# A fused long convolution and maxout FFN: the input's transposes moved from TensorE to the DMA engines

## The chip, the cores and the metric

The kernel runs on one core of a Trainium2 chip. The metric is the device time of one execution in microseconds, the median of several runs. A core has five engines with a queue of instructions each: TensorE (PE, matrix products; its weight loads are listed apart as PEld), VectorE (DVE), ScalarE (ACT), GpSimd (POOL) and SyncE (SP, which here only issues transfers). Sixteen DMA engines carry the transfers. Engines run side by side and wait for one another through semaphores.

## The reference, cut to what matters

```python
def _attn_ref(x, v, pos_emb, w1, w2):             # x, v: (4, 12544, 128)
    h_mlp = np.maximum(pos_emb @ w1, 0.0) @ w2    # a filter per channel
    window = np.exp(-0.01 * np.arange(S))[:, None]
    h_filt = h_mlp * window
    u = x * v
    Uf = np.fft.rfft(u, n=2 * S, axis=1)
    Hf = np.fft.rfft(h_filt, n=2 * S, axis=0)
    y = np.fft.irfft(Uf * Hf[None], n=2 * S, axis=1)[:, :S, :]
    return x * y

def _moe_ref(x, w1, w2, w3, w_out):               # x: (50176, 128), w1..w3: (128, 768)
    h = np.maximum(np.maximum(x @ w1, x @ w2), x @ w3)
    return h @ w_out
```

A causal convolution along the sequence of each channel of `u = x * v`, gated with x, goes through an FFN whose hidden value is the maximum of three products. All arrays are fp32.

## The kernel before

The kernel does the Fourier transforms as matrix products. The 12544 = 128 x 98 positions of a channel lie in a tile as 128 partitions by 98. The first product of the transform contracts over the 98, so each 128 x 98 block is first transposed. A *u* is a set of four channels of one batch, 32 u to a batch. Its steps: load x and v (`u_load`), multiply (`u_mul`), transpose four blocks on TensorE into PSUM and copy them out with ScalarE (`u_turn`), and the first product in two halves (`u_first`).

```python
    def u_load(b, u):
        c, g0 = divmod(u, NG // 4)
        ts = []
        for src in (xr, vr):
            t = (inp0 if b == 0 and u % 2 else inp).tile([P, 4, NB], FP32, tag=f"u{len(ts)}", name="ut")
            nc.sync.dma_start(
                t[:], src[4 * g0:4 * g0 + 4, :, c, b, :].rearrange("g p n -> p g n"))
            ts.append(t)
        us[u] = ts

    def u_mul(u):
        a, v = us[u]
        nc.vector.tensor_tensor(out=a[:], in0=a[:], in1=v[:], op=ALU.mult)

    def turn(u, ps):
        a, _ = us.pop(u)
        for i in range(4):
            nc.tensor.transpose(ps[0:NB, i * P:(i + 1) * P], a[:, i, :], eye[:])

    def u_turn(u):
        if u % 2 == 0:
            uts[u] = uts[u + 1] = utp.tile([NB, 8, 2, 64], FP32, tag="uT", name="uT")
        ps = state["turn"].tile([P, 512], FP32, tag="cv", name="pst")
        turn(u, ps)
        nc.scalar.copy(uts[u][:, 4 * (u % 2):4 * (u % 2) + 4],
                       ps[0:NB, :].rearrange("n (s t r) -> n s r t", s=4, r=2))

    def u_first(u, h, copy=None):
        t = uts[u] if h == 0 else uts.pop(u)
        ps = cps.tile([P, 512], FP32, tag="cv", name="ps1")
        at = 4 * u + 2 * h
        first_halves(ps, [t[:, at % 8 + j] for j in range(2)], f1[:], spec[:, :, :, at:at + 2],
                     copy or copies[h])
```

The convolution of batch 0 is a stage of its own, with the first six u of batch 1 at its end. Then come four batches of FFN tiles, 32 tiles of six steps f each, and beside the FFN of batch b runs the convolution of batch b + 1. `conv_steps` lays it out over the 192 steps (slots) of a batch: first the 32 u (26 for batch 1), then the 45 pairs g of frequencies. An instruction stands in its engine's queue in the order in which the slots name it.

```python
    def conv_steps(b, done):


        out = []

        def at(slot, late, fn, *args):
            out.append((slot, late, len(out), fn, args))

        per_pair = 172 / (NK + 0.4 * (NU - done))
        for u in range(done, NU, 2):
            s = (u - done) * 0.4 * per_pair + 6
            for v in range(2):
                at(max(0, int(s) - 6), 0, u_load, b, u + v)
                at(int(s) - 2 + v, 0, u_mul, u + v)
                at(int(s), 1, u_turn, u + v)
                for h in range(2):
                    at(int(s + 1 + 0.2 * per_pair * (2 * v + h)), 1, u_first, u + v, h)
        s0 = int((NU - done) * 0.4 * per_pair) + 7
        for g in range(NK):
            s = s0 + int(g * per_pair)
            at(s - 5, 0, w_load, g, 0)
            at(s - 3, 0, h_load, g)
            at(s, 1, g_second, g)
            at(s + 1, 0, w_load, g, 1)
            at(s + 1, 0, g_butterfly, g)
            at(s + 2, 0, g_swap, g)
            at(s + 3, 0, g_re, g)
            at(s + 4, 0, g_im, g)
            at(s + 5, 0, g_unfold, g)
            at(s + 6, 1, g_third, b, g)
        slots = {}
        for s, _, _, fn, args in sorted(out, key=lambda r: r[:3]):
            slots.setdefault(s, []).append((fn, args))
        return slots
```

The FFN side: loads for a tile two tiles ahead, and the order of its steps.

```python
    def t_load(b, i):
        zt = hp.tile([N1, 2, 512], FP32, tag="zt", name="zt", bufs=2)
        if b == 0:
            nc.sync.dma_start(
                zt[:], zd[b][:, :, 2 * i:2 * i + 2, :].rearrange("k c t f -> k c (t f)"))
        else:
            for c in range(2):
                nc.sync.dma_start(
                    zt[NK * c:NK * c + NK],
                    zd[b].rearrange("(g a) c t f -> g a c t f", a=2)[
                        :, :, c, 2 * i:2 * i + 2, :].rearrange("g a t f -> g a (t f)"))
        zts[b, i] = zt
        xT = hp.tile([D, 4, NB], FP32, tag="xT", name="xT", bufs=2)
        for c in range(GC):
            nc.sync.dma_start(xT[c * NG:(c + 1) * NG], x[:, 4 * i:4 * i + 4, c, b, :])
        xTs[b, i] = xT
    ...
    def up(i, f):
        rhs = gs[i][:].rearrange("d p n -> d (p n)")
        h = hp.tile([P, N], FP32, tag="hid", name="hid")
        pa = hps.tile([P, 512], FP32, tag="hps", name="pa")
        halves_mm(pa[:, 0:N], w_sb[1][:, f * P:(f + 1) * P], rhs, True, True)
        nc.scalar.activation(h[:], pa[:, 0:N], Relu)
        pb = hps.tile([P, 512], FP32, tag="hps", name="pb")
        halves_mm(pb[:, 0:N], w_sb[2][:, f * P:(f + 1) * P], rhs, True, True)
        nc.vector.tensor_tensor(out=h[:], in0=h[:], in1=pb[:, 0:N], op=ALU.max)
        return h
    ...
    hp = ctx.enter_context(tc.tile_pool(name="hp", bufs=3))
    f4p = hp.tile([N1, 2, NB // 2], FP32, name="f4p", bufs=1)
    nc.scalar.dma_start(f4p[:], f4p_d)
    op_ = ctx.enter_context(tc.tile_pool(name="op", bufs=2))
    wp = ctx.enter_context(tc.tile_pool(name="wp", bufs=3))
    hh = ctx.enter_context(tc.tile_pool(name="hh", bufs=4))
    cvp = ctx.enter_context(tc.tile_pool(name="cvp", bufs=3))
    cps = ctx.enter_context(tc.tile_pool(name="cps", bufs=4, space=PSUM))
    hps = ctx.enter_context(tc.tile_pool(name="hps", bufs=3, space=PSUM))
    ops = ctx.enter_context(tc.tile_pool(name="ops", bufs=1, space=PSUM))
    state = {"turn": cps, "pair": (wp, hh), "cv": (cvp, cps), "xb": 3}


    tiles = [(b, i) for b in range(B) for i in range(NT)]
    late = None
    for n, (b, i) in enumerate(tiles):
        if i == 0:
            beside = {}
            if b + 1 < B:
                beside = conv_steps(b + 1, EARLY if b == 0 else 0)
        if n == 0:
            t_load(*tiles[0])
            t_load(*tiles[1])
            t_last(tiles[0])
        for f in range(NF):

            if i < NT - 2:
                if f == 0:
                    t_load(*tiles[n + 2])
            elif i == NT - 1 and f < 2 and n + 1 + f < len(tiles):
                t_load(*tiles[n + 1 + f])
            h = up((b, i), f)
            if late is not None:
                down(*late)
```

A tile pool with `bufs=3` has three buffers for a tag; the fourth tile of that tag waits until the first one has been used for the last time.

Of the kernel before, what the change touches and what calls it, by code (L numbers as in the profile page):

```python
# [8 lines left out]

FP32 = mybir.dt.float32  # L10
I32 = mybir.dt.int32
ALU = mybir.AluOpType
ACTF = mybir.ActivationFunctionType
PSUM = bass.MemoryType.PSUM
P = 128
# [54 lines left out]
def kernel(  # L70
# [15 lines left out]
    nc = tc.nc  # L86
    NG, _, _, B, NB = x.shape
# [37 lines left out]
    copies = (nc.scalar.copy, nc.vector.tensor_copy)  # L125
# [8 lines left out]
    def first_halves(ps, lhs, table, dst, copy):  # L134


        for i, a in enumerate(lhs):
            for r in range(2):
                for c in range(2):
                    nc.tensor.matmul(  # L140
                        ps[64 * c:64 * c + 64, 256 * i + r * N1:256 * i + (r + 1) * N1],
                        a[:, r, :], table[:, c * N1:(c + 1) * N1],
                        start=(i % 2 == 0 and r == 0), stop=True, skip_group_check=True)
        copy(dst, ps[:].rearrange("p (s m) -> p s m", m=256)[:, :, 0:2 * N1].rearrange(  # L144
            "p s (r k) -> p k r s", r=2))
# [8 lines left out]
    def butterfly(ps, eo, xs):  # L154
        v = ps[:, :].rearrange("p (k r d) -> p k r d", k=2, r=2)
        nc.vector.tensor_tensor(out=xs[:, :, 0, :], in0=eo[:], in1=v[:, :, 0, :], op=ALU.add)
        nc.vector.tensor_tensor(out=xs[:, :, 1, :], in0=eo[:], in1=v[:, :, 0, :],  # L157
                                op=ALU.subtract)

# [10 lines left out]
    def scratch(name, bufs):  # L170
        return sml.tile([P, 2 * HF], I32, tag=name, name=name, bufs=bufs)[:]

    def load_raw(i, h, eng):
        r = scratch("raw", 2)
        if i < 3:
            src = (moe_w1, moe_w2, moe_w3)[i].bitcast(I32).rearrange("(g c) f -> c g f", c=GC)
            for c in range(GC):
                eng.dma_start(r[c * NG:(c + 1) * NG],
                                  src[c][:, h * 2 * HF:(h + 1) * 2 * HF])
        else:  # L180
            src = moe_w_out.bitcast(I32).rearrange("(c p) d -> p c d", p=P)
            eng.dma_start(r.rearrange("p (c d) -> p c d", c=NF // 2),
# [3 lines left out]
    def convert(r, i, h):  # L186
# [12 lines left out]
            lambda: two(out=f2_, in0=lo, scalar1=9, scalar2=ONE,  # L199
                        op0=ALU.logical_shift_right, op1=ALU.bitwise_or),  # L200
            lambda: two(out=f1_, in0=hi, scalar1=12, scalar2=9,
                        op0=ALU.logical_shift_left, op1=ALU.logical_shift_right),
            lambda: one(f1_, f1_, ONE, op=ALU.bitwise_or),
            lambda: two(out=ex, in0=hi, scalar1=1, scalar2=21,
                        op0=ALU.logical_shift_left, op1=ALU.logical_shift_right),
            lambda: two(out=ex, in0=ex, scalar1=896, scalar2=0,
# [16 lines left out]
    utp = ctx.enter_context(tc.tile_pool(name="utp", bufs=2))  # L223
# [91 lines left out]
    NU = NG  # L315
    us, uts, ws, hts, eos, xts, xss, abs_, pss = ({} for _ in range(9))
# [20 lines left out]
    def u_turn(u):  # L337
        if u % 2 == 0:
# [3 lines left out]
        nc.scalar.copy(uts[u][:, 4 * (u % 2):4 * (u % 2) + 4],  # L342
                       ps[0:NB, :].rearrange("n (s t r) -> n s r t", s=4, r=2))

    def u_first(u, h, copy=None):
        t = uts[u] if h == 0 else uts.pop(u)
        ps = cps.tile([P, 512], FP32, tag="cv", name="ps1")
# [3 lines that stand above are left out]
# [69 lines left out]
# [8 lines that stand above are left out]


        per_pair = 172 / (NK + 0.4 * (NU - done))  # L430
        for u in range(done, NU, 2):
            s = (u - done) * 0.4 * per_pair + 6
            for v in range(2):
                at(max(0, int(s) - 6), 0, u_load, b, u + v)
                at(int(s) - 2 + v, 0, u_mul, u + v)
                at(int(s), 1, u_turn, u + v)
                for h in range(2):
                    at(int(s + 1 + 0.2 * per_pair * (2 * v + h)), 1, u_first, u + v, h)
        s0 = int((NU - done) * 0.4 * per_pair) + 7
        for g in range(NK):  # L440
            s = s0 + int(g * per_pair)
            at(s - 5, 0, w_load, g, 0)
# [13 lines that stand above are left out]
# [50 lines left out]
# [10 lines that stand above are left out]
# [68 lines left out]
    for f in range(0, FO, 4):  # L584
        quad([hs[:, f + i] for i in range(4)], f1h[:], specH[:, :, :, f:f + 4])
        u, k = divmod(f // 4, 4)
# [10 lines left out]
    for u in range(0, NU, 2):  # L597
        t = uts.pop(u)
        for v in range(2):
            if u + 4 < NU:  # L600
                u_mul(u + 4 + v)
            at = 4 * (u + v)
# [66 lines left out]
    for s in range(NK + 3):  # L669
# [29 lines left out]
        if NK <= s < NK + 2:  # L699
            for v in range(4):  # L700
                u_first(2 * (s - NK) + v // 2, v % 2, nc.scalar.copy)
# [8 lines left out]
    for u in (4, 5):  # L710
        for h in range(2):
            u_first(u, h)
# [3 lines left out]
    hp = ctx.enter_context(tc.tile_pool(name="hp", bufs=3))  # L716
    f4p = hp.tile([N1, 2, NB // 2], FP32, name="f4p", bufs=1)
    nc.scalar.dma_start(f4p[:], f4p_d)
    op_ = ctx.enter_context(tc.tile_pool(name="op", bufs=2))
    wp = ctx.enter_context(tc.tile_pool(name="wp", bufs=3))  # L720
    hh = ctx.enter_context(tc.tile_pool(name="hh", bufs=4))
# [9 lines left out]
# [19 lines that stand above are left out]
            late = ((b, i), f, h)  # L750
            if f == 3 and n + 1 < len(tiles):
                t_last(tiles[n + 1])
            s = i * NF + f
            run(beside.pop(s, ()))
            if s == NT * NF - 1:
                assert not beside, sorted(beside)
# [38 lines left out]
```

## Time and profile before

| | |
|---|---|
| median of 3 runs | 2464.02 us (2463.47 to 2464.71) |
| span of the profiled execution | 2462.5 us |
| PE busy | 2445.7 us, 99% |
| DVE busy | 1343.9 us, 55% |
| ACT busy | 1010.5 us, 41% |
| POOL busy | 62.5 us, 3% |
| TensorE clock granted | 0.999 of full speed |
| DMA | 384.61 MB, mean 156 GB/s |
| `pst` transposes (line 335) | 512 on PE, 273 ns median each, overlapped |
| copy of `pst` by ACT (line 342) | 96 of 98x512 fp32, 588 ns each |

A row of the profile names the line of the kernel, the engine, the operation, the tile written and the tiles read with their shapes, how often it ran, its busy time and the mean of one. PE has its work overlapped, so a matmul's duration is longer than its share of the span; the chain that ended last gives that share. "Issue to landing" is the time from the moment a queue begins to issue a transfer until all of it has arrived. "Idle before" is the time in which an engine waited ahead of an instruction, with the releaser it waited for.

### The profile page before, as it was taken

To read this page: it belongs to the slowest core of one execution; us is meant where nothing else is said; L and a number is where in the kernel's file an instruction comes from. 1 tells how busy PE (TensorE), PEld (TensorE's weight loads), DVE (VectorE), ACT (ScalarE), POOL (GpSimd) and SP (SyncE) were. 2 spreads that over 40 slices of the span, in tenths; PEclk is the share of its full clock that TensorE was granted. 3 is DMA by queue.
4 is the path that set the end of the run, shared out by engine and by line. 5 is a ranking of instruction groups with operands and counts; after the bars stand their busy time and mean duration, and the time that the engine had idled before them with its cause. 6 is when DMAs were issued, how large, how long until landed. Compare 5 with 4: busy or idle time off the path is not lost.

```text
span 2462.5 us, 63180 instructions
## 1 busy us (share of the span) xinstructions
PE 2445.7 (99%) x26449; PEld 1476.2 (60%) x26449; DVE 1343.9 (55%) x2764; ACT 1010.5 (41%) x1981; POOL 62.5 (3%) x121
## 2 busy tenths in 40 slices
PE   8999999999999999999999999999999999999999
PEld 7988866655555556655555556655555554444444
DVE  5588833466666634366666743456766652222322
ACT  2688833334444433344444433344444432222222
POOL 2022200000000000000000000000000000000000
PEclk9999999999999999999999999999999999999999
DMA  7779855677777545577777735477777732222221
GB/s 160 182 240 274 265 127 122 166 200 192 193 185 205 145 105 121 124 197 201 209 207 200 201 86 133 115 186 198 206 206 203 204 105 55 64 58 57 61 55 36
DMA packets 449511, 384.61 MB, mean 156 GB/s; under 512 B 295204, under 2 KB 341341, under 8 KB 449225
## 3 DMA queue, kind: packets, MB, share of 16 engines
q1 hardware_dynamic: 326720, 291.64, 46.6%
q10 hardware_dynamic: 117129, 74.31, 10.1%
q0 software_dynamic: 5376, 14.62, 2.1%
q8 instruction: 208, 3.41, 0.6%
q14 instruction: 78, 0.64, 0.1%
HBM read 295.76 MB, written 84.67 MB: 154 GB/s over the span
## 4 chain that ended last, share of the span: by engine, by line
PE 98%; DVE 1%; issue 0%; ACT 0%; ACTq 0%; DVEq 0%
PE ops L131 24%; PE pa L131 21%; PE pb L131 20%; PE ps L131 13%; PE ps L140 7%; PE yps L131 5%; PE sps L654 3%; PE pst L335 3%; PE gps L640 1%; PE pm L302 1%; PE pw L131 1%; ACT ht L659 0%; DVE xs L391 0%; DVE zs L416 0%; DVE xt L392 0%
## 5 line engine op out<-in xcount | busy, mean ns | idle before, releaser
L514 DVE TENSOR_TENSOR hid<-hid,pb 128x392 f32<-128x392 f32 x768 | 431.3, 562 | 775.9 <-PE pb L131 462.7
L511 ACT ACTIVATE hid<-pa 128x392 f32<-128x392 f32 x768 | 382.5, 498 | 634.6 <-PE pa L131 600.0
L131 PE MATMUL pa<-gt,w_sb 128*64 128x392 f32 x3072 | 639.4, 495 | 0.7 <-DVE gt L499 0.7
L131 PE MATMUL ops<-hid,wo_sb 128*64 128x392 f32 x3072 | 637.6, 494 | 0.1
L131 PE MATMUL pb<-gt,w_sb 128*64 128x392 f32 x3072 | 635.8, 492 | 1.8 <-ACT hid L511 1.8
L131 PEld LDWEIGHTS pb<-gt,w_sb 128*64 128x64 f32 x3072 | 219.2, 137 | 289.2 <-issue 270.4
L131 PEld LDWEIGHTS ops<-hid,wo_sb 128*64 128x64 f32 x3072 | 215.9, 137 | 291.8 <-issue 232.6
L131 PEld LDWEIGHTS pa<-gt,w_sb 128*64 128x64 f32 x3072 | 198.8, 137 | 160.4 <-issue 101.0
L131 PEld LDWEIGHTS ps<-ab,wt 128*64 128x64 f32 x2880 | 167.1, 137 | 56.5 <-issue 33.7
L140 PEld LDWEIGHTS ps<-f,uT 98*64 98x64 f32 x4096 | 172.9, 137 | 36.5 <-issue 33.4
L131 PE MATMUL ps<-ab,wt 128*64 128x128 f32 x2880 | 189.5, 274 | 0.9 <-DVE ab L398 0.6
L131 PE MATMUL ps<-spec,wt 128*64 128x128 f32 x2880 | 187.9, 273 | 0.0
L140 PE MATMUL ps<-f,uT 98*64 98x90 f32 x4096 | 181.3, 241 | 0.0
L131 PEld LDWEIGHTS ps<-spec,wt 128*64 128x64 f32 x2880 | 163.8, 137 | 6.0 <-issue 5.6
L381 ACT ACTIVATE xs<-xt 64x512 f32<-64x512 f32 x180 | 113.1, 628 | 127.1 <-DVE xt L157 120.7
L144 ACT COPY spec<-ps 128x360 f32<-128x360 f32 (+1 forms) x132 | 71.6, 545 | 171.6 <-PE ps L140 171.4
L162 ACT COPY eo<-ps 128x256 f32<-128x256 f32 x180 | 67.1, 373 | 173.8 <-PE pa L131 150.8
L398 DVE TENSOR_TENSOR ab<-xt 128x256 f32<-128x256 f32 x360 | 136.0, 419 | 1.6
L387 DVE TENSOR_TENSOR xt<-xt,ht 128x512 f32<-128x512 f32 x180 | 123.5, 686 | 14.4 <-ACT ht L659 14.1
L392 DVE TENSOR_TENSOR xt<-xt,xs 128x512 f32<-128x512 f32 x180 | 124.6, 692 | 6.3
L416 DVE TENSOR_TENSOR zs<-ps,z 128x256 f32<-128x256 f32 x270 | 101.8, 419 | 47.4 <-ACT z L414 45.4
L131 PEld LDWEIGHTS yps<-f4p,zt 90*64 90x64 f32 x3072 | 106.1, 138 | 35.6 <-issue 34.0
(81 smaller groups left out, 1744.4 us busy)
## 6 DMA issues: line engine op xcount, KB each, us to landing
wt<-wt_const SPq DMA_DIRECT2D x360, 256.0 KB, 4.5
ht<-hd SPq DMA_DIRECT2D x270, 256.0 KB, 5.1
zd<-zs ACTq DMA_DIRECT2D x180, 256.0 KB, 4.3
zt<-zd SPq DMA_DIRECT2D x192, 180.0 KB, 3.8
ut<-in_xr_dram SPq DMA_DIRECT2D x128, 196.0 KB, 3.8
ut<-in_vr_dram SPq DMA_DIRECT2D x128, 196.0 KB, 4.1
xT<-in_x_dram SPq DMA_DIRECT2D x512, 49.0 KB, 3.1
out_dram<-ot ACTq DMA_DIRECT2D x128, 196.0 KB, 3.9
```

Source lines behind the costliest of these rows:

```text
L131: nc.tensor.matmul(out[64 * h:64 * h + 64], lhsT[:, 64 * h:64 * h + 64], rhs, start=start, stop=stop, skip_group_check=True)
L140: nc.tensor.matmul(ps[64 * c:64 * c + 64, 256 * i + r * N1:256 * i + (r + 1) * N1], a[:, r, :], table[:, c * N1:(c + 1) * N1], start=(i % ...
L144: copy(dst, ps[:].rearrange("p (s m) -> p s m", m=256)[:, :, 0:2 * N1].rearrange("p s (r k) -> p k r s", r=2))
L335: nc.tensor.transpose(ps[0:NB, i * P:(i + 1) * P], a[:, i, :], eye[:])
L381: nc.scalar.mul(xs[0:64], xt[64:128], -1.0)
L387: nc.vector.tensor_tensor(out=xt[:], in0=xt[:], in1=hts[g][:, 0], op=ALU.mult)
L392: nc.vector.tensor_tensor(out=xt[:], in0=xt[:], in1=xs[:], op=ALU.add)
L398: nc.vector.tensor_tensor(out=ab[:, :, q, :], in0=y[:, :, 0, :], in1=y[:, :, 1, :], op=op)
L416: nc.vector.tensor_tensor(out=zs[:, a], in0=ps[:, 0:256], in1=z1[:], op=op)
L511: nc.scalar.activation(h[:], pa[:, 0:N], Relu)
L514: nc.vector.tensor_tensor(out=h[:], in0=h[:], in1=pb[:, 0:N], op=ALU.max)
L654: nc.tensor.matmul(ps[64 * h:64 * h + 64, (2 * c + k) * 2 * D:(2 * c + k + 1) * 2 * D], G[:, k, c], w2x[:].rearrange("p s d -> p (s d)"), ...
```

## The change: the transposes beside the FFN by DMA

Beside the FFN the four TensorE transposes of a u are replaced. The transposing DMA works here on 2-byte elements, so GpSimd takes the fp32 product apart into a plane of low and a plane of high 16-bit halves (`u_planes`), each padded from 98 to 128 columns; one transposing DMA on SyncE's queue turns the eight 128 x 128 blocks (`u_dma`); ScalarE puts the low halves and VectorE the high halves back into the fp32 tile (`u_join`). The bits are kept as they are. Batch 0 and the first six u of batch 1 stay on TensorE. Each u is now laid out by itself rather than in pairs, with leads for the new steps. It is meant to relieve TensorE of work that isn't part of the products.

```diff
--- before.py
+++ after.py
@@ -9,6 +9,7 @@
 
 FP32 = mybir.dt.float32
 I32 = mybir.dt.int32
+U16 = mybir.dt.uint16
 ALU = mybir.AluOpType
 ACTF = mybir.ActivationFunctionType
 PSUM = bass.MemoryType.PSUM
@@ -342,6 +343,32 @@
         nc.scalar.copy(uts[u][:, 4 * (u % 2):4 * (u % 2) + 4],
                        ps[0:NB, :].rearrange("n (s t r) -> n s r t", s=4, r=2))
 
+
+
+    def u_planes(u):
+        a, _ = us.pop(u)
+        pl_ = planes[u % 2]
+        nc.gpsimd.tensor_copy(
+            pl_[:, :, :, 0:NB], a[:].bitcast(U16).rearrange("p s (n h) -> p h s n", h=2))
+        us[u] = pl_
+
+    def u_dma(u):
+        t = hp.tile([P, 8, P], U16, tag="turned", name="turned", bufs=2)
+        nc.sync.dma_start_transpose(
+            out=t[:], in_=us.pop(u)[:].rearrange("p h s n -> p (h s n)"))
+        us[u] = t
+
+    def u_join(u):
+        if u % 2 == 0:
+            uts[u] = uts[u + 1] = utp.tile([NB, 8, 2, 64], FP32, tag="uT", name="uT")
+        t = us.pop(u)
+        for h in range(2):
+            copies[h](
+                uts[u][:, 4 * (u % 2):4 * (u % 2) + 4].rearrange(
+                    "n s r t -> n (s r t)").bitcast(U16).rearrange(
+                    "n (s r t h) -> n h s r t", h=2, r=2, t=64)[:, h],
+                t[0:NB, 4 * h:4 * h + 4].rearrange("n s (t r) -> n s r t", r=2))
+
     def u_first(u, h, copy=None):
         t = uts[u] if h == 0 else uts.pop(u)
         ps = cps.tile([P, 512], FP32, tag="cv", name="ps1")
@@ -428,15 +455,16 @@
 
 
         per_pair = 172 / (NK + 0.4 * (NU - done))
-        for u in range(done, NU, 2):
-            s = (u - done) * 0.4 * per_pair + 6
-            for v in range(2):
-                at(max(0, int(s) - 6), 0, u_load, b, u + v)
-                at(int(s) - 2 + v, 0, u_mul, u + v)
-                at(int(s), 1, u_turn, u + v)
-                for h in range(2):
-                    at(int(s + 1 + 0.2 * per_pair * (2 * v + h)), 1, u_first, u + v, h)
-        s0 = int((NU - done) * 0.4 * per_pair) + 7
+        for u in range(done, NU):
+            s = (u - done) * 0.4 * per_pair + 7
+            at(max(0, int(s) - 7), 0, u_load, b, u)
+            at(int(s) - 4, 0, u_mul, u)
+            at(int(s) - 3, 0, u_planes, u)
+            at(int(s) - 2, 0, u_dma, u)
+            at(int(s), 0, u_join, u)
+            for h in range(2):
+                at(int(s + 1 + 0.2 * per_pair * h), 1, u_first, u, h)
+        s0 = int((NU - done) * 0.4 * per_pair) + 8
         for g in range(NK):
             s = s0 + int(g * per_pair)
             at(s - 5, 0, w_load, g, 0)
@@ -716,6 +744,9 @@
     hp = ctx.enter_context(tc.tile_pool(name="hp", bufs=3))
     f4p = hp.tile([N1, 2, NB // 2], FP32, name="f4p", bufs=1)
     nc.scalar.dma_start(f4p[:], f4p_d)
+    planes = [hp.tile([P, 2, 4, P], U16, name=f"planes{i}", bufs=1) for i in range(2)]
+    for t in planes:
+        nc.gpsimd.memset(t[:].rearrange("p h s n -> p (h s n)"), 0)
     op_ = ctx.enter_context(tc.tile_pool(name="op", bufs=2))
     wp = ctx.enter_context(tc.tile_pool(name="wp", bufs=3))
     hh = ctx.enter_context(tc.tile_pool(name="hh", bufs=4))
```

## The prediction, made before the changed kernel had run

> **What bounds the kernel now.** I read the page first: busy time, then the chain that ended last.
>
> ```profile
> PE 2445.7 (99%) x26449; PEld 1476.2 (60%) x26449; DVE 1343.9 (55%) x2764; ACT 1010.5 (41%) x1981; POOL 62.5 (3%) x121
> ...
> PE 98%; DVE 1%; issue 0%; ACT 0%; ACTq 0%; DVEq 0%
> PE ops L131 24%; PE pa L131 21%; PE pb L131 20%; PE ps L131 13%; PE ps L140 7%; PE yps L131 5%; PE sps L654 3%; PE pst L335 3%; PE gps L640 1%; PE pm L302 1%; PE pw L131 1%; ACT ht L659 0%; DVE xs L391 0%; DVE zs L416 0%; DVE xt L392 0%
> ```
>
> TensorE is the bound nearly throughout, and the transposes (`pst`, line 335) are 3% of the chain. So work taken off TensorE is worth its whole length, as long as no other engine is made to be waited for. Next, where the transposes lie. The instructions on `pst` stand in four stretches: the prologue up to about 450 us (batch 0, and batch 1's u), about 905 to 1040 (batch 2), and 1477 to 1610 us (batch 3). I call such a stretch an input phase. The busy table of the last two:
>
> ```profile
> 905.00:1040.00 135.00, 135.00 (x1717) 88.46 (x1718) 52.55 (x101) 52.00 (x104) 0.00 (x0) 1.00 0.54 125
> 1477.00:1610.00 133.00, 133.00 (x1704) 87.25 (x1702) 52.69 (x100) 50.23 (x100) 0.00 (x0) 1.00 0.56 129
> ```
>
> The columns are the stretch, its length, then busy time (and count) of PE, PEld, DVE, ACT and POOL, the clock, the DMA engines' share and GB/s. TensorE has no gap, POOL does nothing, DVE and ACT are 39% busy, the DMA engines 54%. A batch has 32 units u, so one takes 135/32 = 4.2 us. What a transpose costs is read from the chain in order of time (start, length, what), in a stretch of that phase:
>
> ```profile
> 947.53 1.01 PE pst L335 x8
> 948.54 0.81 PE pa L131 x4
> 949.35 0.66 PE pb L131 x4
> ...
> 951.91 0.66 PE pa L131 x4
> ```
>
> Eight transposes (two u) take 1.01 us, and the `pa` group after them 0.81 instead of 0.66. A pair of u thus costs 1.16 us. Last, the transfers of the same 135 us, and what they take from issue to landing:
>
> ```profile
> DMA packets 38701, 16.84 MB, mean 125 GB/s; under 512 B 37443, under 2 KB 37443, under 8 KB 38685
> ...
> L323 SPq DMA_DIRECT2D ut<-in_xr_dram x29: 367/368/539, 905.6 to 1031.4; - x29
> ...
> DMA to landing us min/median/max: 2.7/3.8/5.4
> ```
>
> Most packets are small. 0.54 x 16 engines x 135 us / 38,701 = 30 ns of an engine for each. An issue holds the sync queue for 0.37 us.
>
> [...]The trace has 273 ns for one fp32 transpose, pipelined to 0.13[...]; no DMA transpose is in the trace.[...]
>
> **The change, part by part.** It concerns 32 + 32 u of batches 2 and 3 and 26 of batch 1 (six are done earlier): 90.
>
> Removed from TensorE: 45 pairs x 1.16 us = 52 us, all on the path. That is the ceiling of the gain, 2.1%: 2464 - 52 = 2412. A u then needs 4.2 - 0.58 = 3.6 us of TensorE.
>
> ACT's copy from PSUM, 588 ns each, 90 of them, goes. In its place ACT and DVE each get a copy of 98 x 512 halves per u, an estimated 0.6 us by the same element count: ACT the same, DVE 90 x 0.6 = 54 us more, on an engine 39% busy. Nothing of that is on the path by itself.
>
> Added: per u a POOL copy (1.5 us), a 256 KB transpose through the sync queue, and waits. For its latency L I take the 3.8 us median of the plain 196 KB loads, [...]plus a little for busier engines: 6 us, an estimate, with 4 to 10 thinkable.
>
> Now the new chain. The plane buffers are two and the turned buffers two, so `u_planes(u)` waits for transpose u-2 to land, and transpose u for planes u. That alone gives two u per L + 1.5 + some 0.4 of semaphores = 7.9 us, or 4.0 per u. But the sync queue is in order, and in the changed program's queue a period of five u stands thus (T transpose, L the two loads of a u, X the zt and xT loads of an FFN tile):
>
> ```
> X  T6 T7 L11 T8 L12 T9 L13 T10 L14 L15  X  T11 T12 ...
> ```
>
> A load L(k) goes into the buffer of u = k-3 (three buffers) and so waits for planes k-3. Hence: T6 lands, planes 8, T8 lands, planes 10, T10 lands, planes 12, then L15 may issue, six X loads behind it, and only then T11.[...] So five u need 3 x (6 + 1.5 + 0.4) + 4.4 = 28 us, or 5.6 per u, against 4.2 before and 3.6 of TensorE's work. The join waits in ACT's and DVE's order, ahead of the FFN's relu and maximum; TensorE has three `hps` buffers, about one FFN step of slack, and then stands still. Full cost: 90 x (5.6 - 4.2) = +126 us, 2590. TensorE's slack and the gaps at phase ends (the tail needs no loads, the fill has seven slots of lead) soften it; I take off a third: +90, so 2555.
>
> **Rivals.** *All hidden*: with L = 4 the period is (3 x 5.9 + 4.4) / 5 = 4.4[...]. For it: [...]POOL is empty, DVE and ACT have room, and the steps have leads of two to four slots. Against it: even the fastest plain load needs 2.7 us and the ring has three of them in series. It makes 2412 to 2450. *The DMA engines become the bound*: 128 partitions x 8 rows of 256 bytes are 1024 small pieces; at 30 ns each over 16 engines 1.9 us per u, on top of 0.54 x 4.2 = 2.3. That is 4.2, the period of before: a gain of nothing, 2464, and longer queues that lengthen L. If the pieces are smaller on the writing side it is worse.[...] *POOL slower than estimated*: each us more is 0.6 us per u, +54 us.
>
> **Range and chances.** The middle is 2555. The range from 2430 (nearly all hidden) to 2740 (L about 8, little slack) should hold 8 in 10. Faster by over 2% would be below 2415, within 3 us of the ceiling: 0.05. Within 2% (2415 to 2513) needs L of some 4.5 us or less, or much slack: 0.29. Slower: 0.66.
>
> **What would show each step.** The `pst` instructions of the three phases gone from TensorE, 52 us less of its busy time; POOL copies of about 1.5 us; transposes [...]about 6 us to landing; ACT's and DVE's joins waiting for the DMA, for about 2 us per u in the three phases; TensorE's share there down from 100% to some 65%; the phases at 170 to 180 us instead of 135; everything outside them as before. I am wrong if joins hardly wait (then L, or the ring, is shorter than I think), if DMA share there goes to 0.9 (then it is the engines, not the ring), or if time is lost outside the phases.

## The result, and the profile after

| | before | after |
|---|---|---|
| median | 2464.36 us (2463.47 to 2465.51) | 2482.4 us (2475.33 to 2487.03) |
| ratio | | 1.007 (1.0045 to 1.0096) |
| PE busy in the profiled run | 2445.7 us | 2418.8 us |
| POOL busy | 62.5 us | 181.6 us |
| mean TensorE clock granted | 0.999 | 0.990 |

The change made the kernel 18 us slower. The forecast was 91 us, with a range of 2430 to 2740: the direction and the range held, the size did not. The prediction had given 0.29 to a time within 2%. The page of the changed kernel, busy time, then the chain that ended last:

```profile
PE 2418.8 (98%) x26089; PEld 1453.6 (59%) x26089; DVE 1380.5 (56%) x2854; ACT 1017.1 (41%) x1981; POOL 181.6 (7%) x213
...
PE 90%; DMA 6%; SPq 1%; ACT 1%; DVE 1%; issue 1%; ACTq 0%; POOL 0%; DVEq 0%; POOLq 0%
PE ops L132 22%; PE pa L132 19%; PE pb L132 19%; PE ps L132 13%; PE ps L141 6%; PE yps L132 5%; DMA turned<-planes 5%; PE sps L682 3%; PE pm L303 1%; PE gps L668 1%; SPq L504 1%; PE pst L336 1%; DMA zt<-zd 1%; ACT uT L366 1%; DMA specH<-in_pos_emb_dram 0%
```

`pst` went from 3% of the chain to 1%, and `turned<-planes`, the transposing DMA, came in with 5%. TensorE is no longer alone on the chain. The busy table shows where, in the same stretch of batch 2 as before (columns: stretch, length, PE, PEld, DVE, ACT, POOL, clock, DMA share, GB/s):

```profile
905.00:1040.00 135.00, 114.45 (x1432) 72.91 (x1428) 58.84 (x121) 48.75 (x93) 37.11 (x28) 0.92 0.88 164
```

TensorE is busy 114 of 135 us where it had no gap, the clock is 0.92 instead of 1.00, and the DMA engines' share rose from 0.54 to 0.88. The instructions on the tile `turned` give the cost of each part and who waited (us, times):

```profile
L357 SPq DMA_TRANSPOSE turned<-planes x90: 1232/1267/2622, 335.5 to 1626.3; - x90
L366 ACT COPY uT<-turned x90: 769/784/806, 339.6 to 1630.3; 98x512 uint16<-98x512 uint16 x90
L366 DVE COPY uT<-turned x90: 445/458/1086, 339.6 to 1630.9; 98x512 uint16<-98x512 uint16 x90
...
  POOL planes L351: 278.1, 67
  ACT uT L366: 194.8, 68
  DVE uT L366: 143.3, 59
...
DMA to landing us min/median/max: 3.0/3.8/6.5
```

An issue takes 1.27 us of the sync queue, and a transpose has landed 3.8 us after its issue began, about as long as a plain load (3.9 for the loads of u in the same run, 3.3 for x and 3.7 for v in batch 2; medians). GpSimd waits for transposes in 67 of 90 copies, and ScalarE stands at the join 195 us, 2.2 us per u.

Time went by phase. I take the start of the last first product of each input phase as a mark: 457.0, 1048.4 and 1617.8 us before; 451.7, 1057.5 and 1638.9 after. So batch 1's phase gained 5 us, batch 2's stretch lost 14, batch 3's lost 12, and the rest of the span (2462.5 against 2479.2) gave back 4.

What the transposes wait for shows where the sync queue and GpSimd stand in order of time (start, length, what). This is once around, from T6 and T7 (the first line) to T11 in the prediction's numbering; the transposes, loads and copies between are left out at the dots:

```profile
956.24 2.66 SPq L357 DMA_TRANSPOSE turned<-planes  x2
...
962.32 1.24 SPq L357 DMA_TRANSPOSE turned<-planes  x1
...
965.99 1.48 POOL L351 COPY planes<-ut 128x784 uint16<-128x784 uint16 x1 [4.03 <-DMA turned<-planes]
...
969.18 1.24 SPq L357 DMA_TRANSPOSE turned<-planes  x1
...
972.98 1.49 POOL L351 COPY planes<-ut 128x784 uint16<-128x784 uint16 x1 [1.05 <-DMA turned<-planes]
...
974.91 0.51 SPq L324 DMA_DIRECT2D ut<-in_vr_dram  x1
975.52 1.74 SPq L497 DMA_DIRECT2D zt<-zd  x2
977.30 2.90 SPq L504 DMA_DIRECT2D xT<-in_x_dram  x4
980.30 1.27 SPq L357 DMA_TRANSPOSE turned<-planes  x1
```

From T6 to T8, from T8 to T10 and from T10 to the zt load go 6.1, 6.9 and 6.3 us: a transpose lands, GpSimd takes the planes of the u after next apart (the number in brackets is its wait for that transpose), the loads behind that go out, and only then the next transpose. Two zt issues and four xT issues take 4.7 us more. This is the ring of the prediction, 24.1 us for five u. The chain that ended last, from the zt load on:

```profile
975.19 0.64 PE ps L141 x16
975.83 0.56 SPq L497
...
978.84 1.35 SPq L504
...
980.30 3.36 DMA turned<-planes
...
983.81 1.49 POOL planes L351
...
985.31 0.41 SPq L324
...
985.77 0.50 SPq L324
...
986.36 3.81 DMA turned<-planes
```

The zt load, which the queue reached at 975.52, waited until 975.83 for TensorE. So TensorE is part of the loop as well, but by little: between 890 and 1060 us the queue's zt loads waited 6.5 us for TensorE, and its loads of u 40.3 us for GpSimd's copies.

### The profile page after: what moved, and what is told of

It is laid out like the page before. It is cut to its first block, busy times and chain, and to the rows that moved or that the text cites. A ratio compares the mean times of both kernels' runs of the same rounds, so it can differ in the third digit from the quotient of the medians.

```text
span 2479.2 us, 63072 instructions
## 1 busy us (share of the span) xinstructions
PE 2418.8 (98%) x26089; PEld 1453.6 (59%) x26089; DVE 1380.5 (56%) x2854; ACT 1017.1 (41%) x1981; POOL 181.6 (7%) x213
## 4 chain that ended last, share of the span: by engine, by line
PE 90%; DMA 6%; SPq 1%; ACT 1%; DVE 1%; issue 1%; ACTq 0%; POOL 0%; DVEq 0%; POOLq 0%
PE ops L132 22%; PE pa L132 19%; PE pb L132 19%; PE ps L132 13%; PE ps L141 6%; PE yps L132 5%; DMA turned<-planes 5%; PE sps L682 3%; PE pm L303 1%; PE gps L668 1%; SPq L504 1%; PE pst L336 1%; DMA zt<-zd 1%; ACT uT L366 1%; DMA specH<-in_pos_emb_dram 0%
## 5 line engine op out<-in xcount | busy, mean ns | idle before, releaser
L132 PEld LDWEIGHTS pa<-gt,w_sb 128*64 128x64 f32 x3072 | 204.8, 138 | 166.1 <-issue 101.4
L141 PE MATMUL ps<-f,uT 98*64 98x90 f32 x4096 | 191.4, 247 | 45.5 <-ACT uT L366 43.8
L141 PEld LDWEIGHTS ps<-f,uT 98*64 98x64 f32 x4096 | 178.9, 141 | 86.9 <-ACT uT L366 53.2
L351 POOL COPY planes<-ut 128x784 uint16<-128x784 uint16 x90 | 117.1, 1308 | 1201.0 <-DVE ut L331 911.0
L366 ACT COPY uT<-turned 98x512 uint16<-98x512 uint16 x90 | 70.5, 784 | 197.6 <-DMA turned<-planes 194.8
```

What stands on the lines that cost most here:

```text
L132: nc.tensor.matmul(out[64 * h:64 * h + 64], lhsT[:, 64 * h:64 * h + 64], rhs, start=start, stop=stop, skip_group_check=True)
L141: nc.tensor.matmul(ps[64 * c:64 * c + 64, 256 * i + r * N1:256 * i + (r + 1) * N1], a[:, r, :], table[:, c * N1:(c + 1) * N1], start=(i % ...
L351: nc.gpsimd.tensor_copy(pl_[:, :, :, 0:NB], a[:].bitcast(U16).rearrange("p s (n h) -> p h s n", h=2))
L366: copies[h](uts[u][:, 4 * (u % 2):4 * (u % 2) + 4].rearrange("n s r t -> n (s r t)").bitcast(U16).rearrange("n (s r t h) -> n h s r t", h= ...
```

## The experiments

All times are medians of runs on the same chip as their kernel before (2463.9 to 2465.2 us). **Ring theory**: two plane buffers and the loads' place ahead of the transposes on the in-order sync queue make the transposes run after one another (the first expectations say: wherever the loads stand; `load6` below decides between the two). **Queue theory**: it is the block of six FFN loads in front of one transpose in five. **DMA theory**: the DMA engines are full.

**Spread the xT loads (`spread`).**

```diff
-        for c in range(GC):
-            nc.sync.dma_start(xT[c * NG:(c + 1) * NG], x[:, 4 * i:4 * i + 4, c, b, :])
+        for c in range(GC):
+            owed.append((b, i, c))      # one is issued at each later FFN step
```

> The changed kernel, but the four xT loads of an FFN tile are issued one per FFN step instead of together with the two zt loads. Queue theory (a transpose stands on the sync queue behind a block of six FFN loads, some 4.7 us of issue, once per five u, and that is when the joins wait long): the block shrinks to two issues, the waits of the joins on the DMA fall from 338 us to under 200 us, the kernel comes to 2440 to 2465 us. Ring theory (two plane buffers make transposes wait for each other, wherever the loads stand): joins wait about as before, 2475 to 2490 us. DMA theory (the engines are full, the bytes are the same): 2475 to 2490 us.

Measured: 2477.7 us, ratio 1.0052 (1.0035 to 1.007). ScalarE's wait at the joins is 196.7 us, against 194.8. The block by itself is not the cause. That its issue time lies on the ring wherever it stands would explain this; it was not tested by itself.

**A third buffer of each (`deep`), of the planes alone (`planes3`), of the turned tiles alone (`turned3`).**

```diff
-        pl_ = planes[u % 2]
+        pl_ = planes[u % 3]                                      # deep, planes3 (and three tiles)
-        t = hp.tile([P, 8, P], U16, tag="turned", name="turned", bufs=2)
+        t = hp.tile([P, 8, P], U16, tag="turned", name="turned", bufs=3)   # deep, turned3
```

> The changed kernel with three plane buffers and three turned buffers instead of two of each. Ring theory: copy and transpose of three u may be under way, the joins' waits for the DMA fall by more than half, 2430 to 2455 us. Queue theory: the six loads still stand in front of one transpose in five, but that transpose no longer waits for the copies behind it in time: a small gain, 2465 to 2480 us. DMA theory: no change, 2475 to 2490 us.

> The changed kernel with three plane buffers, and two turned buffers as before. If the ring that costs is the one over the plane buffers (copy of u waits until transpose u-2 has landed), this alone gives nearly all of what three of both gave: 2428 to 2440 us, joins' waits under 200 us. If it is the turned buffers (transpose of u waits for the joins of u-2), this gives little: 2470 to 2485 us. DMA theory: 2475 to 2490 us.

> The changed kernel with three turned buffers and the two plane buffers as before. Ring over the plane buffers: no gain, 2475 to 2488 us. If a third buffer of either kind would do (the ring runs over both), 2430 to 2450 us.

Measured: `deep` 2431.2 us (0.9859, 0.9844 to 0.9875), `planes3` 2427.6 us (0.9858, 0.9842 to 0.9875), `turned3` 2480.6 us (1.0061, 1.0046 to 1.0076). The whole gain comes from the third plane buffer and none from the third turned tile, so the ring runs over the planes. The waits of both engines for transposes fell from 338.1 us to 172.6 in `deep`, a little less than the half that was expected, and to 195.2 in `planes3`. Batch 2's stretch with `planes3`:

```profile
905.00:1040.00 135.00, 133.87 (x1716) 83.07 (x1714) 68.99 (x141) 59.55 (x114) 26.00 (x26) 0.99 1.01 197
```

TensorE is busy again, the clock is back at 0.99, and the DMA share is higher (1.01; above 1, so the times of packets overlap in it) while the kernel is 55 us faster than the changed one.

**The layout with TensorE transposes (`sched`), and with a later multiplication (`sched2`).**

```diff
-            at(int(s) - 4, 0, u_mul, u)
+            at(int(s) - 1, 0, u_mul, u)     # sched2 only
-            at(int(s) - 3, 0, u_planes, u)
-            at(int(s) - 2, 0, u_dma, u)
-            at(int(s), 0, u_join, u)
+            at(int(s), 1, u_turn, u)
```

> The changed kernel's layout of the steps (each u by itself, one slot later), but with the four TensorE transposes per u of the kernel before in place of planes, DMA and join. All theories say the layout is worth nothing by itself: 2460 to 2470 us, TensorE 100% busy in the three phases. If it is 2475 or more, the loss comes from the layout and not from the transposes by DMA.

> The changed kernel's layout by single u with TensorE transposes, and the multiplication three slots later than in the earlier run of this layout, so that VectorE does not stand at a load that waits for the transpose of the same slot. If that standing was the whole loss of the earlier run (2700 us), this comes back to 2460 to 2475 us. If the layout by single u costs by itself, it stays over 2500 us.

Measured: `sched` 2700.3 us (1.0955), a plain miss for every theory. In the changed kernel GpSimd's copy frees a load buffer three slots ahead of the join. With the transpose on TensorE the buffer is held to the last slot, so the multiplication, which stands earlier in VectorE's order, waits for a load that waits for that transpose:

```profile
DVE ut L331 <- DMA ut<-in_vr_dram: 438.0, 84, 10.3
```

(us in total, times, longest.) With the multiplication moved, `sched2` takes 2475.3 us (1.0046, 1.0031 to 1.0061). The layout by single u then still costs 11 us, which the prediction had at nothing; TensorE is busy 2456.9 us, 11 more than before. The chain shows where (of the kernel before, the prediction shows 1.01 us for eight transposes):

```profile
951.20 0.57 PE pst L336 x4
951.77 0.81 PE pa L132 x4
```

Four transposes by themselves take 0.57 us, more than half of eight, and the `pa` group behind every four is 0.15 us longer, as it was only once per pair before: an estimated 90 x 0.72 - 45 x 1.16 = 13 us. So this is a cost of TensorE's transposes standing singly. The changed kernel has none beside the FFN, and `no_dma` below, with the same layout, shows no such cost.

**Transposing DMAs that nobody reads (`side`, `side2`, `side3`).**

```diff
+            at(int(s) - 3, 0, u_planes, u)  # side; in side2 at int(s)
+            at(int(s) - 2, 0, u_dma, u)     # side, side3; in side2 at int(s)
             at(int(s), 1, u_turn, u)        # the product comes from TensorE's transposes
-            out=t[:], in_=us.pop(u)[:].rearrange("p h s n -> p (h s n)"))
+            out=t[:], in_=planes[u % 3][:].rearrange("p h s n -> p (h s n)"))   # side3: no copy
```

> The TensorE transposes of the run before in this list stay and feed the product; beside them GpSimd's copies and the 90 transposing DMAs are done as well (three buffers of each), but nothing reads what they turn. DMA theory: the engines' share in the phases goes from 0.54 to about 0.9 and the FFN's and the u loads come late, so TensorE waits: 2480 us or more. Queue and ring theories: nobody waits for a transpose, so 2462 to 2472 us.

> The run before in this list plus GpSimd's copies and the 90 transposing DMAs (three buffers of each) that nobody reads. DMA theory (engines full): 20 us or more above the run before in this list, and loads that land a microsecond or more later. Ring theory: within 8 us of it, although the DMA engines' share in the phases nearly doubles.

> The layout by single u with TensorE transposes and the late multiplication (2475 us), and beside it the 90 transposing DMAs of buffers that were cleared once: no copy by GpSimd ahead of them, nothing reads what they turn, so neither the copies nor the loads wait for them. Ring theory: the bytes and the 1.25 us of issue alone cost nothing, 2473 to 2483 us, with the DMA engines' share in the phases near 0.9. DMA theory: 2490 us or more, and loads that land later make VectorE's multiplication wait.

`side` has the layout of `sched`, `side2` and `side3` that of `sched2`. Measured: `side` 2710.9 us (1.1001), which says little beside the 2700 of its own layout. `side2` 2597.2 us (1.0536), against 2475 without: my assumption that nobody waits was false. GpSimd's copy also reads the load buffer, so a load waits for the copy, the copy for a transpose, and the next transpose stands behind the load. The chain of `side2` shows that ring bare:

```profile
947.41 4.15 DMA turned<-planes
951.61 0.08 issue
951.68 0.85 POOL planes L351
952.55 0.37 SPq L324
952.97 0.51 SPq L324
953.52 3.58 DMA turned<-planes
```

6.1 us from one transpose to the next, with the DMA engines at a share of only 0.58 (900 to 1050 us). `side3` takes the copy away and with it the ring: 2475.8 us (1.0042, 1.0025 to 1.0059), the time of `sched2` within its interval. The stretch of batch 2 in `sched2`:

```profile
905.00:1040.00 135.00, 135.00 (x1638) 84.27 (x1636) 52.27 (x100) 49.95 (x97) 0.00 (x0) 1.00 0.49 114
```

and in `side3`:

```profile
905.00:1040.00 135.00, 135.00 (x1640) 84.33 (x1638) 52.09 (x100) 49.88 (x97) 0.00 (x0) 1.00 0.87 167
```

The share goes from 0.49 to 0.87 and TensorE does not notice, although the loads of u land later: 3.2 and 3.6 us (medians for x and v, 905 to 1040 us) instead of 2.8 and 3.1. The DMA theory falls.

**No transposing DMA (`no_dma`).** The joins read a cleared tile; u_dma is left out.

```diff
-            at(int(s) - 2, 0, u_dma, u)
-        t = us.pop(u)
+        us.pop(u)
+        t = still
```

> The changed kernel without the transposing DMAs; the joins read a tile that was cleared once, so the convolutions of batches 1 (from u 6) to 3 are computed from zeros. GpSimd's copies and the joins stay. All theories: TensorE busy throughout, 2408 to 2418 us; this is the floor of the change. Over 2425 us would mean that the copies or the joins cost by themselves.

Measured: 2410.7 us (0.9778, 0.9762 to 0.9794), PE busy 2391.7 us, so 54 us less than before. This kernel computes the convolutions of most of batches 1 to 3 from zeros. Copies and joins cost nothing by themselves, and the ceiling of the prediction (2412 us) stands.

**The joins one slot later (`lead`), with spread loads (`lead_spread`).**

```diff
-            at(int(s), 0, u_join, u)
+            at(int(s) + 1, 0, u_join, u)    # u_first and the pairs g also one slot later
```

> Three buffers of each, and the join and the first products one slot (some 3 us) later. If what is left of the waits is latency alone, a further slot hides most of it: joins wait under 60 us, the clock stays at 1.0, and the time comes to the ceiling of the prediction, 2412 to 2422 us. If the DMA engines or the ring set the pace of the phase, the joins wait as long as with three buffers alone: 2426 to 2436 us.

> Three buffers of each, join and first products one slot later (2419 us), and the xT loads one per FFN step. Queue theory: with the ring gone, what is left of the joins' waits comes from the block of six loads, so 2412 to 2417 us. If the block is hidden by then, 2417 to 2422 us.

Measured: `lead` 2419.1 us (0.9819, 0.9804 to 0.9833), 8 us above the floor and faster than both kernels, before and after. ScalarE still stands 80.0 us at the joins, more than the 60 expected, but TensorE's matmuls wait only 7.8 us for it. `lead_spread` 2429.5 us (0.9855, 0.9841 to 0.987) is slower than `lead`, against both expectations; ScalarE's wait at the joins is 106.1 us there. Why is open.

**The loads one slot later, at two buffers (`load6`) and with `lead` (`lead6`).**

```diff
-            at(max(0, int(s) - 7), 0, u_load, b, u)
+            at(max(0, int(s) - 6), 0, u_load, b, u)
```

On the sync queue that moves every load of a u behind one more transpose. T is a transpose, L the loads of a u, X the FFN tile's loads:

```
changed kernel:  T5 L9 L10 X T6 T7 L11 T8 L12 T9 L13 T10 L14 L15 X T11
load6:           T5 L8 L9  X T6 L10 T7 T8 L11 T9 L12 T10 L13 L14 X T11
```

> The changed kernel with two buffers of each, and only the loads of a u one slot later. On the sync queue a transpose then stands behind the load that waits for its own planes, no longer behind the one that waits for the planes of the next u. If the ring that costs is made by the two plane buffers together with that place on the queue, five u need about 2.5 rounds of transpose, copy and load issue instead of 3, (2.5 x 6.3 + 4.8) / 5 = 4.1 us per u instead of 4.8: 2430 to 2462 us. If the two plane buffers alone make it, wherever the loads stand: 2475 to 2488 us.

> Three buffers of each, join and first products one slot later (2419 us), and the loads one slot later as well. If the place of the loads matters only as long as two buffers make a ring: 2415 to 2423 us. If the transposes still wait behind the loads: 2411 to 2415 us, the floor.

Measured: `load6` 2432.6 us (0.9861, 0.9845 to 0.9878). With the two plane buffers of the changed kernel, the place of the loads alone is worth 50 us, as much as a third buffer. The joins of batch 2 run from 896.9 to 1025.1 us, 4.14 us per u; 4.1 was expected. That the two agree so well is partly luck: the expectation had GpSimd's copy at its 1.5 us, and in `load6` its median is 0.84; and without any transposing DMA a u takes 3.80 (`no_dma`, 887.7 to 1005.4 us over 31). So the ring needs both: two buffers, and a load ahead of the transpose that waits for the planes of the next u. `lead6` 2432.9 us (0.9869, 0.9854 to 0.9883) was expected at 2411 to 2423 and is 14 us slower than `lead`. Its joins hardly wait (25.1 us on ScalarE), but VectorE's multiplication waits 145.7 us for loads, against 85.2 in `lead`, and TensorE 13.6 us for VectorE in the FFN. These waits point to the later load as what comes too late once the ring is gone.

## Why the prediction was half right

**What TensorE gives up: right.** 52 us and a floor of 2412 were worked out; `no_dma` has 2411.

**The ring: right in its shape.** The order T6 T7 L11 T8 ... L15 X T11, with three rounds and one block X for five u, is what the sync queue shows, and `planes3`, `turned3` and `load6` each touch it where it was said to run.

**The step that failed: L = 6 us, the latency of a transpose in the ring's sum.** The prediction put it 2.2 us above the 3.8 us of a plain load; that was the author's estimate, which no trace of the kernel before shows, as it has no transposing DMA. Measured from the start of its issue, the transpose takes 3.8 us altogether, with 1.27 of issue in it. The prediction had said itself that a time within 2% needs an L of some 4.5 us or less. GpSimd's copy was put at 1.5, which no trace of before shows either, and is 1.48 (median), but by luck: in `no_dma` the same copy takes 0.84, and the prediction had nothing of what goes with the longer copies (last section). Semaphores and the two load issues behind the copy make 1.0 or somewhat more (1.2 in the chain shown: 983.66 to 983.81 and 985.30 to 986.36 us) instead of the estimated 0.4; X, estimated at 4.4, is 4.7 from the start of its first issue, at 975.52 us. So five u need 3 x (3.8 + 1.5 + 1.0) + 4.7 = 23.6 us, or 4.7 per u, where 5.6 was put. The turn shown above took 24.1. Measured from join to join: 4.83 (899.3 to 1048.9 us over 31) and 4.72 (1484.0 to 1630.3) in batches 2 and 3.

**Two smaller terms.** The period of before is not 4.2 but 4.4: ScalarE's copies of `pst` stand in pairs, so 30 u lie between the first and the last start:

```profile
L342 ACT COPY uT<-pst x32: 585/588/591, 906.1 to 1038.9; 98x512 f32<-98x512 f32 x32
```

And the third that was taken off for slack was not there in batches 2 and 3, whose period is the ring's. There (4.83 - 4.4) x 32 + (4.72 - 4.4) x 32 = 24 us, about the loss that the marks show (14 + 12 = 26). Batch 1 has a period of 4.26 (339.6 to 446.1 us over 25) against 4.6 before (336.9 to 447.5 over 24) and gained; it has one zt load per FFN tile instead of two and another spacing of u. That difference was not tested.

**Rivals.** That a transpose is much slower than a plain load was thinkable, with an L of up to 10 us: the 3.8 us for eight blocks rule that out. How long the moving alone takes, no run isolates. The small pieces were counted rightly: 95,041 more packets in 90 transposes, 1056 each, against 1024. That they would set the pace was wrong (`side3`). "All hidden" failed only through the ring; with the ring opened it is nearly reached (`lead`, 2419.1 us).

**What was to be seen.** The joins wait 2.2 us per u, as said. TensorE's share in batch 2's phase is 85%, not 65. Its busy time fell by 27 us and not by 52, because part of its work ran at a lower clock: (0.999 - 0.990) x 2479 us is an estimated 22 us of the missing 25, and with `planes3` (mean clock 0.998) the busy time is 2398.0 us. The DMA engines' share went to 0.88, which the prediction had named as a sign against its ring; `side3` reaches 0.87 without any loss, so the sign itself was wrong.

## What to carry to other kernels

When a new step gets buffers of its own, follow the ring through the in-order queue as well: what stands ahead of the transfer there, and whose release does it wait for? A load issued one step too early can hold back the transfer behind it as much as a missing buffer (here its place was worth 50 us and the third plane buffer 55), and moving it costs no memory. A transfer that is fast enough one by one (3.8 us) may still lose if its rounds run in series (24.1 us for five u); engines with a high busy share are not the proof of a bound (0.87 in `side3`, at the time of `sched2`), and adding the same bytes with nobody waiting tells.

## What the runs showed of the hardware

TensorE ran slower after some of its waits; the prediction had left that out. In the changed kernel the 32 first products that follow a gap of 3.2 us, and the `pa` group behind them, take twice as long as their likes a few us later:

```profile
960.39 2.50 PE ps L141 x32
962.88 1.29 PE pa L132 x4
964.17 0.66 PE pb L132 x4
...
965.49 1.24 PE ps L141 x32
```

The granted clock of the 10 us from 960 is 0.83, and after a gap of 2.6 us at 984.5 the 32 products took 2.67 us. The length of the gap does not decide alone: in `side2` TensorE stood still for 2.8 us until 963.0 us, and its clock in the 15 us after that is 1.00; the `pa` group behind it takes 0.88 us in the timeline, and the one behind a gap of 2.7 us until 978.5 us takes 1.58. How much of the 18 us is this and how much the wait itself was not separated (the 22 us estimated above are the most it can be, as TensorE also stood idle): every run that shortened the waits also raised the clock (mean 0.996 to 0.998 in `deep`, `planes3`, `lead`, `lead_spread`, `load6` and `lead6`, against 0.990).

GpSimd's copy of 128 x 784 halves has a median of 1482 ns in the changed kernel and 843 ns in `side2`. In the changed kernel 62 of the 90 copies overlap both a join and a multiplication by VectorE, and they take 1.48 us or more; the other 28 take 0.84 to 1.16. In `planes3` only 17 overlap both, and the median is 0.84. That VectorE's join and multiplication hold the copy up is what these counts suggest; no run changes them alone. It matters for the ring: a landing transpose releases the copy and the join together (one at 983.66 us starts them at 983.81 and 983.68, with a multiplication at 984.03). Three copies of 0.84 us instead of 1.48 would take an estimated 1.9 us off the 24.1, which is 4.4 per u, the period of before. Both `planes3` and `load6` shortened the copies along with the waits, so these two shares of their gain are not separated.
